# Attention and FFN on one core: another replayed order, and another order of several waits

## The chip, the core and the metric

The kernel runs on one core of one Trainium2 chip. A core has five engines with instruction queues of their own: TensorE (PE in the profile; its weight loads are PEld), VectorE (DVE), ScalarE (ACT), GpSimd (POOL) and SyncE (SP), which here only issues transfers. They meet through semaphores alone. Matrix products land in PSUM, which this kernel uses as eight banks of 512 fp32 columns; everything else lies in SBUF. The metric is the device time of one execution in microseconds, median of several; lower is better.

## What is computed

From the reference, for one sequence of S = 2048 positions with D = 640, 32 heads of 20 columns that share one key and one value head, and F = 1728:

```python
xn = _layernorm(x)
q = (xn @ wq).reshape(B, S, 32, 20)          # 32 query heads
k, v = xn @ wk, xn @ wv                      # one head for all
p = _softmax(einsum("bhqd,bkd->bhqk", q, k) * 20 ** -0.5)
a = einsum("bhqk,bkd->bhqd", p, v) ... @ wo
f = silu(xn @ w1) @ w2
return x + a + f
```

## The kernel before

**Tiling.** Queries are cut into 4 chunks of 512 columns, heads into 8 groups of 4, keys into 16 tiles of 128. So there are 32 (chunk, group) pairs with 16 key tiles of 4 heads each: 2048 score tiles of 128 keys x 512 queries. A score tile is one matmul with 32 rows (L1211); four of them, one for each head, run side by side in the four row groups of PE. A PV step multiplies the exponentials of one key tile with v for 4 heads, side by side in four column groups (L1336); it sums into the bank of its group.

**Two ways to an exponential.** The ACT path: one ACTIVATE (L1301, "exp") reads one to three neighbouring banks and writes bf16. The DVE path, for whole key tiles: a conversion on DVE (L1533, "p1") for each of the 4 heads turns scores into integers whose bits are an approximate exponential; two integer shifts of the whole tile (128 x 2048) give two more approximations, each on POOL (L1572) or on DVE (L1577); three PV steps, one for each with its own scaled copy of v, then sum them. So a tile on the DVE path needs 4 conversions, 2 shifts and 3 PV steps, one on the ACT path 4 banks of exp and 1 PV step.

**Jobs.** Between the attention run the other products as jobs, all with matmuls of L536 in four column groups: "q" (queries of a later chunk, 5 pieces a chunk, one DVE copy, then DMAs that spread its rows over heads), "h" (FFN up, 14 pieces a chunk, the last one shared by two chunks; a tanh on ACT at L862 and a product on DVE at L865), "out" (FFN down and attention output, half a token tile, 320 columns, one DVE operation at L992), and for the last chunk "y", "w", "sum", "spread" and "fin".

**Where the order comes from.** `build` does not write instructions. It makes operations (`Op`) with an estimated duration and a list of what they wait for, and a planner commits them one by one to the five engines; `emit` then writes the queues. Until 36 us of planned time, `step_pe` chooses by rules. From there on (`replay["on"]`), `follow` (L2094) reads the string `ORDER` (L116), three letters a step, which fixes what PE does next, and `follow_other` the strings `OTHERS` (L180), which fix the order of the kinds of operations on ACT, DVE and POOL. In `ORDER`, `S`/`s` is a score set for ACT (second letter: number and spacing of banks; third: first bank), `D` to `K` one score tile for DVE (head, bank; the letter also says which shifts go to DVE), `a`/`d` a PV step of ACT's or of DVE's path, `n` the start of a job, `m` its next matmuls. When the string ends, the rules decide the rest.

**Durations in the planner.** `t_act`, `t_dve`, `t_mc` (L250 ff.) and the tables `WAY*`, `*_END`, `SWITCH` estimate how long operations and the ways between engines take. In the replayed part the estimates do not choose what comes next on PE; they decide, in `est` and `commit`, when an operation is thought to start and end, and with it how the queues of SP and the unlisted operations fall in.

**Waits.** `emit` keeps for each engine what it already knows of the others and writes the missing waits ahead of an operation, in a list sorted by the position of the awaited operation in its own engine's queue, last first (L2306). An instruction carries one wait, and further ones become semaphore instructions ahead of it, which the profile shows at L2339.

Of the kernel before, what the change touches and what calls it, by code (L numbers as in the profile page):

```python
# [10 lines left out]
I16 = mybir.dt.int16  # L11
# [9 lines left out]
HG = 4  # L21
# [30 lines left out]
WAY = {("act", "dve"): 32.0, ("dve", "pool"): 84.0, ("pe", "act"): 41.0, ("pe", "dve"): 72.0}  # L52
# [5 lines left out]
ACT_END = 104.0  # L58
DVE_END = 85.0
# [22 lines left out]
SWITCH = {"s": 97.0, "p": 98.0, "f": 98.0}  # L82
SPRIO = 0.5
# [28 lines left out]
def rule(n):  # L112
# [4 lines left out]
    "D32D13S14a97nq6m00m00D25S20m00m00S22D34aa7S20Dd5nh6m00D04D22S13m00m00m00S20S14Dd5G33nh2m00m00m00m00S25D00D31nh4m00m00m00m00ab7S25D20S13nh2m00m00m00m00"  # L117
    "S25Dc1D14nh0m00m00m00m00ac7S21D23s25ad7ae7af7d04d14S31D30d34d24D85D16S17a04d44d64S10S21D33d54a14d94S25E20D97d74dc4S22D01d84df4S25D20D97a24da4nh1m00S22"
    "E30m00D05D26S17m00m00S22E30a34a44db4S25Dc7di4dd4S22D20dl4nh1m00S35de4S10D32Dc3m00m00dg4dj4m00S25E12S17nq0m00m00m00m00dh4S22D35D81a54a64S26D10a74S22D75"
    "nh1m00m00m00m00S25D20S17nh2m00m00dk4m00m00S25D11S13dm4nh7m00m00m00dn4m00S30D85G26nh3m00m00m00m00S24D27s20D12a06a16a26a36d06S24D33Da7d16d36S20D02d26d66"  # L120
    "S23D35a46d46S20E12D87a56d96d56S33D32d86S20D17a66dc6nh2m00S23Dc5D77m00m00m00da6S20E25d76nh3m00m00S24Dc7m00S20D12m00a76nq7m00S24D72m00m00db6m00S20D23a86"
    "S24D82a96df6S20D13E27de6dd6nh2S24D33m00D10E21S17m00m00m00S33S10nh7dh6m00m00m00dg6m00S11S24Db3a02a12d02d32d12S20D13D26d62d22S24D07a22a32S13S20Da6a42d52"
    "nh7m00m00S23D05D16m00m00a52d92d82S20D33De4a62S25d42d72da2S20D33De7dc2S25D04a72nh3m00S20D77m00S24E16m00m00S17D10De1a82db2S24E06a92dd2S20D17de2nh3m00S24"
    "D06m00m00aa2m00S26S10Da1F34nh5m00m00m00m00S22D06a07d07d37S20D34d27d17S22D15a17d67S20Da4D36d57d97S22D05a27d77S20Da4nh6m00m00S22D15m00a37S20D34d87D05E12"
    "S13m00nh4m00m00S20Dd5a47m00m00S22D06d47a57dc7S20D26Dd5da7df7S22E34db7S20D26a67dd7S24D02nh3m00m00S20Dd6m00a77S24E32de7dg7m00S20D26a87nq2m00m00S25D04m00"
    "m00S20D93a97dh7d04S25D32d14S20D23a04d34d24S25D02E37d64S20D93a14nh2m00S25D07m00D23S10D81m00m00a24S35D33nh0m00m00m00m00a34d54S31s25D17d94d74dc4d84d44D20"
    "S21E33a44da4Dc7S25D10a54db4S21D23nh7m00E35Dc0S16m00m00m00S21D13a64df4S25D30dd4nh3m00S21E27m00Dc0S15D26a74m00m00S21D17a84de4S25D30nh7m00S21D83m00m00S25"
    "D20a94dh4S31dg4m00a05d05d35d65D14s16S31nq0m00m00m00m00S26D34a15d25S21D90D23a25d15d45D04S26d55d95S20D92D63a35d75S26D34d85nq2m00S20Dd3m00S26D04m00m00S20"
    "D63a45a55S26E32D04dc5da5db5S20Dd2D63a65df5S26E34nq2m00S20Dd3m00m00S26D04m00a75S20D63a85dd5S26E32de5dg5S20D94a95dh5S22D06E37nq4m00S20D25m00m00S22D06m00"
    "a07d07S20D95d37d67S22D34D06d27S20D25a17a27S32G36d57a37d97S20S25d87dc7a47d17S22Da4F00D11d47d77a57S24Dc6G30S22da7D11S24Dc6a67df7D20s31db7S24D56a77E30s31"  # L130
    "Dc6de7D20S24G36a87S30a97dh7S34dd7dg7nq3m00m00m00m00S20D22a07d07S25D14D83a17d37S20D32d17d47S25D14D83a27d27S20D22d67E34s25D13a37d57S20D22d97a47S23D85G36"
    "S20D22d77da7a57S23D15dc7S20E36d87S22Dc4D15a67df7S20D26db7S22Dc4D55a77S20S16F34a87S22D25de7S20E34F86D15dh7S32a97dd7S20dg7d06d36S32D35G27a06a16S20D95d66"
    "S22D04D37d16no5m00m00m00S20E24m00m00S22D87m00m00m00D14S20m00m00m00d26m00S22S14D87m00m00m00m00m00a26a36S30D33m00a46a56d96d56S24D27d46S20D32Dc3d76da6d86"
    "S24D12E27a66dc6S20D33db6S24D12no7m00m00m00m00S20Dc3m00m00m00m00S24E22a76S20D33m00m00m00m00m00m00S32D25m00m00m00m00a86a96S20E15df6S22Da4D37dd6dg6S20D05"
    "no4m00de6S22Da7m00m00dh6S20D15m00m00m00m00S22D37Da6m00m00m00a05m00S20D07m00a15S22D76d05d15S20D17d35d25S22Da6m00m00a25S20D07m00m00m00m00S22D76a35d65S20"
    "E14D07d55d45S22De6a45a55S20E14D07a65d95S22D36d75d85S20E14Dc7dc5da5S22D26df5db5D14S20D87a75a85a95no2S23E36de5S20D17m00m00m00m00m00S23S26m00m00m00m00m00"
    "m00dh5S20D23D34m00m00m00m00dd5S26D83m00m00m00S20D24dg5a03S26D12a13a23a33S20E34Da5d03d33S26D02a43d13S20D34d63S35E12a53d23nq4m00S20Dc2m00m00m00S25D17d93"
    "d53S20D32d73dc3d43S24D26Dd7a63D00S11S12a73da3d83S24D26a83S20E37Dc2db3nq6m00S24D17m00m00m00S30D87a93aa3S24D26de3no7m00m00m00S30D56m00m00m00m00m00m00m00"
    "S24D36m00m00m00S20D22m00m00dd3S24E36m00m00m00S20D92a03d03d33S24D06d13d23S20D27D92a13a23S34a33d43S20D37D22a43d63d93d53S24D06Dd7a53d73S20E32da3dc3S24D06"
    "a63d83S20D27E32df3no6m00m00m00S24Dc7m00m00S20D22m00m00m00S24D17m00m00m00m00db3S30E37m00m00m00m00m00m00S24D97a73S20D06D32a83dd3no7de3S24E26m00m00S20D82"  # L140
# [12 lines left out]
    "dg0no3m00m00m00S21D87m00m00m00S24D26m00m00S21D57m00m00m00m00dh0S34D37m00m00m00m00m00m00a00S21D27s25E33D84a10a20a30a40S21D13D27d00d30S25E34d10d20S21Dd3"
    "D27d60d40S25D04d90d50S21Dd3a50a60S24E36D07dc0d70d80S21D23a70S34nq7m00m00m00m00S21E33a80db0S24Dc6D17a90D23S11S12da0dd0de0S24D86D57no1m00m00m00m00m00S22"
    "D36m00S24D87m00m00m00m00m00m00S22S16D37m00m00m00m00m00m00aa0S32E25a07a17d07d37S20D16d27d67S22D24E35a27d17S20D86a37d47S22D24D35d57d97S20E16a47d77S22De4"
    "dc7d87S20D06D15a57df7S22D34no6m00db7S20Dc5m00m00m00m00a67S22S24m00m00m00m00m00m00de7S20D22D33m00m00m00m00da7S24E12m00m00m00S20Da3a77a87S24D02D16a97dd7"
    "S20E33dg7no2m00m00S25D84m00m00S20D23m00m00m00dh7m00S34D13m00m00m00S20D37m00m00m00m00m00m00m00S33Da6a07a17a27d07S20D02d37d17S23D35d67d27S20E12D86a37a47"
    "S24D23d97d57d47S20D12Dc6a57d77S24D33d87dc7S20D12Dc6a67da7S24D23df7db7S20D52nq6m00S24E33m00m00m00S20Dc2a77S23D25a87de7dd7S30D56a97E35D24S13dg7no6m00m00"
# [91 lines left out]
def t_act(n):  # L250
    return 64.0 + 0.8333 * n
# [6 lines left out]
def t_mc(n):  # L258
    return n / 2.4 + (9.0 if n >= 512 else 4.0)
# [44 lines left out]
class Sched:  # L304
# [42 lines left out]
    def turn(self, mode):  # L347
        return SWITCH[mode] if mode != self.pe_mode else 0.0

# [2057 lines left out]
```

## Time and profile before

| | us |
|---|---|
| median of 3 runs | 671.09 (670.93 to 672.82) |
| profiled execution, its own time | 671.75 |
| its span, first to last instruction | 669.9 |
| PE busy, 9919 matmuls | 660.0 |
| ACT busy, 750 instructions | 652.7 |
| DVE busy, 1103 instructions | 632.8 |
| POOL busy, 322 instructions | 535.5 |

The profile is of one execution. A busy time is the union of an engine's instructions, which overlap at their ends: neighbours on ACT by some 0.15 us, on DVE by some 0.08. So a busy share near 100% does not tell how much waiting is left; steps from start to start do. "Stretches" are rows of busy time by engine between two times. "The chain" follows the last instruction back to whatever released each step.

### The profile page before, as it was taken

The page shows a single profiled execution, that of the slowest core. Times are in us where ns is not written, and L with a number is a line of the kernel's source. Part 1 is how long each engine was busy: PE and PEld are TensorE (multiplying, and loading weights), DVE is VectorE, ACT ScalarE, POOL GpSimd, SP SyncE. Part 2 cuts the span into 40 slices and gives each one's busy share as a digit, 9 for nine tenths or more (in the row PEclk, how much of TensorE's full clock was granted, in tenths as well). Part 3 has the DMA queues.
Part 4 walks back from the last instruction along what each step waited for, and adds up shares of the span by engine and source line. Part 5 has one row for each costly group of instructions (what it writes and reads, how often), then busy time and mean ns, then how long its engine had stood idle before and what let it go on. Part 6 is the DMA issues. An engine that isn't in the chain of part 4 may idle for free.

```text
span 669.9 us, 22826 instructions
## 1 busy us (share of the span) xinstructions
PE 660.0 (99%) x9919; PEld 240.1 (36%) x9919; DVE 632.8 (94%) x1103; ACT 652.7 (97%) x750; POOL 535.5 (80%) x322
## 2 busy tenths in 40 slices
PE   8999999999999999999999999999999999999997
PEld 5433332332223333333332333333333333344434
DVE  7899999999999999999999999999999999988885
ACT  6999999999999999999999999999999999999995
POOL 6647879888777888977889788878878888778863
PEclk9999999999999999999999999999999999999999
DMA  8652202222131223223222231122422202242021
GB/s 229 169 198 19 30 18 23 23 27 31 26 35 24 34 19 40 30 31 37 63 23 26 26 40 26 24 32 33 77 21 24 21 21 33 22 79 24 9 23 41
DMA packets 34242, 28.99 MB, mean 43 GB/s; under 512 B 15486, under 2 KB 29662, under 8 KB 34142
## 3 DMA queue, kind: packets, MB, share of 16 engines
q1 hardware_dynamic: 33854, 27.20, 26.6%
q8 instruction: 78, 1.28, 0.8%
q10 hardware_dynamic: 288, 0.33, 0.1%
q14 instruction: 22, 0.18, 0.1%
HBM read 11.09 MB, written 2.62 MB: 20 GB/s over the span
## 4 chain that ended last, share of the span: by engine, by line
PE 79%; ACT 10%; DVE 8%; POOL 1%; issue 0%; DMA 0%; DVEq 0%; POOLq 0%; ACTq 0%
PE psall L1336 28%; PE psall L1211 25%; PE psall L536 24%; ACT sbt L1301 9%; DVE sbt L1533 5%; DVE sbt L1577 1%; POOL sbt L1572 1%; PE psall L710 1%; PE psall L684 1%; DVE sbt L782 0%; DVE sbt L1385 0%; DMA sbt<-in_A_x_dram 0%; PE psall L1150 0%; PE psall L1132 0%; DVE sbt L1100 0%
## 5 line engine op out<-in xcount | busy, mean ns | idle before, releaser
L1301 ACT ACTIVATE sbt<-psall 128x1024 bf16<-128x1024 f32 (+2 forms) x677 | 622.7, 1042 | 3.7 <-PE psall L1211 2.7
L1572 POOL TENSOR_SCALAR sbt<-sbt 128x2048 int16<-128x2048 int16 x250 | 474.3, 1897 | 94.3 <-DVE sbt L1577 25.1
L1533 DVE TENSOR_SCALAR sbt<-psall 128x512 int16<-128x512 f32 x720 | 458.1, 681 | 21.0 <-PE psall L1211 16.4
L1336 PE MATMUL psall<-sbt 128*32 128x512 bf16 x3488 | 274.4, 384 | 0.8 <-POOL sbt L1572 0.2
L1211 PE MATMUL psall<-sbt 32*128 32x512 bf16 x2048 | 251.1, 384 | 2.8 <-ACT sbt L1301 1.1
L536 PE MATMUL psall<-sbt 128*32 128x512 bf16 (+4 forms) x3904 | 216.9, 331 | 0.1
L1211 PEld LDWEIGHTS psall<-sbt 32*128 32x128 bf16 x2048 | 69.1, 91 | 222.0 <-ACT sbt L1301 137.3
L536 PEld LDWEIGHTS psall<-sbt 128*32 128x32 bf16 x3904 | 84.5, 95 | 82.6 <-issue 40.2
L1336 PEld LDWEIGHTS psall<-sbt 128*32 128x32 bf16 x3488 | 71.0, 94 | 108.3 <-issue 73.9
L1577 DVE TENSOR_SCALAR sbt<-sbt 128x2048 int16<-128x2048 int16 x110 | 74.6, 710 | 0.2
L949 POOL TENSOR_TENSOR sbt<-sbt 128x512 bf16<-128x512 f32 x30 | 38.3, 1275 | 19.6 <-DVE sbt L1577 17.3
L865 DVE SCALAR_TENSOR_TENSOR sbt<-sbt,psall 128x512 bf16<-128x512 bf16 x52 | 35.2, 677 | 0.2
L862 ACT ACTIVATE sbt<-psall 128x512 bf16<-128x512 f32 x52 | 32.9, 633 | 0.0
L1385 DVE COPY sbt<-psall 128x512 f32<-128x512 f32 x31 | 21.2, 682 | 0.8 <-PE psall L1336 0.6
L782 DVE TENSOR_SCALAR sbt<-psall 128x512 bf16<-128x512 f32 x20 | 13.6, 680 | 0.5 <-PE psall L536 0.3
L661 POOL TENSOR_TENSOR sbt<-sbt 128x2 f32<-128x2 f32 x8 | 5.7, 708 | 8.6 <-DVE sbt L659 8.2
L992 DVE SCALAR_TENSOR_TENSOR sbt<-psall,sbt 128x320 bf16<-128x320 f32 x24 | 11.6, 485 | 0.6 <-PE psall L536 0.6
L674 POOL TENSOR_SCALAR sbt<-sbt 128x640 bf16<-128x640 bf16 x12 | 10.4, 874 | 1.5 <-DVE sbt L666 1.5
L652 DVE BATCH_NORM_STATS2 sbt<-sbt 128x6 f32<-128x320 bf16 x14 | 6.6, 473 | 2.0 <-DMA sbt<-in_A_x_dram 1.9
L684 PE MATMUL psall<-sbt 128*128 128x128 bf16 x80 | 6.9, 220 | 1.1 <-DVE sbt L677 1.1
L1835 PE MATMUL psall<-sbt 128*32 128x256 bf16 x144 | 6.8, 353 | 1.2 <-DVE sbt L576 1.2
L696 DVE COPY sbt<-psall 128x640 bf16<-128x640 bf16 x14 | 6.4, 482 | 1.0 <-PE psall L684 1.0
(59 smaller groups left out, 97.8 us busy)
## 6 DMA issues: line engine op xcount, KB each, us to landing
sbt<-sbt SPq DMA_DIRECT2D x120, 64.0 KB, 3.8
sbt<-in_A_x_dram SPq DMA_DIRECT2D x28, 160.0 KB, 3.9
sbt<-sbt SPq DMA_DIRECT2D x213, 20.0 KB
out_dram<-sbt SPq DMA_DIRECT2D x14, 160.0 KB, 1.9
sbt<-in_B_w_dram SPq DMA_DIRECT2D x1, 2160.0 KB, 12.2
sbt<-in_B_w_dram SPq DMA_DIRECT2D x1, 2080.0 KB, 8.1
sbt<-sbt SPq DMA_DIRECT2D x75, 8.0 KB
sbt<-in_A_wq_dram SPq DMA_DIRECT2D x1, 800.0 KB, 6.3
```

The source lines that it names most:

```text
L536: ins = pe.matmul(ps[j * SLOT:(j + 1) * SLOT, b * BANK + off:b * BANK + off + n], w[:, j * SLOT:(j + 1) * SLOT], x, start=start, stop=stop ...
L782: op = Op("dve", lambda v: v.tensor_scalar_mul(q_st[:, st, :], bk(job.bank), QSCALE), t_dve(512), DVE_END, pre=[job.ready], writes=[res("q ...
L862: t = Op("act", lambda a: a.activation(t_buf[0:rows, ts, :], bk(job.bank, 0, QW, rows=rows), AF.Tanh, scale=0.5), t_act(512), ACT_END, pre ...
L865: u = Op("dve", lambda v: v.scalar_tensor_tensor(out=hT[par][0:rows, fk, :], in0=t_buf[0:rows, ts, :], scalar=1.0, in1=bk(job.bank, 0, QW, ...
L949: nm = pool(lambda e: e.tensor_tensor(oU[:, us, :], U_sb[:, us, :], Rrep, ALU.mult), 1356.0, POOL_END, pre=[uc] + lc + pack_op.get(divmod( ...
L1211: return pe.matmul(bk(b), kT_rep[i * SLOT:(i + 1) * SLOT, kt * P:(kt + 1) * P], qT[i * SLOT:(i + 1) * SLOT, g % NQ, :], start=True, stop=T ...
L1301: return a.activation(Ebuf[:, es * QW:es * QW + w], ps[:, buf[0] * BANK:buf[0] * BANK + w], AF.Exp, scale=ESCALE)
L1336: ins = pe.matmul(ps[i * SLOT:(i + 1) * SLOT, ub * BANK:ub * BANK + QW], lhsT, rhs, start=(first and k < HG), stop=(last and k >= len(lst) ...
L1385: return v.tensor_copy(U_sb[:, us, :], bk(ub))
L1533: p1 = Op("dve", lambda v: v.tensor_scalar(z16[:, i * QW:(i + 1) * QW], bk(job.bank), ZBIAS, 0.0, ALU.add, ALU.max), t_dve(QW) + 2.0, DVE_ ...
L1572: op = pool(lambda v, t=t, j=j, zin=zin: v.tensor_scalar(t.bitcast(I16), zin, float(SHIFT[j]), 1.0, ALU.add, ALU.mult), POOL_SHIFT, POOL_E ...
L1577: op = dve(lambda v, t=t, j=j, zin=zin: v.tensor_scalar_add(t.bitcast(I16), zin, float(SHIFT[j])), t_dve(N, 4), prio=SPRIO - 0.01 * j, **args)
```

## The change

Three things change.

1. **`ORDER` and `OTHERS` are other strings**, 3128 steps instead of 3144. What they hold, counted:

| in the replayed part | before | after |
|---|---|---|
| score sets for ACT of 1 / 2 / 3 banks | 88 / 504 / 62 | 76 / 528 / 54 |
| banks on the ACT path | 1282 | 1294 |
| score tiles on the DVE path | 716 | 704 |
| shifts on DVE / on POOL | 110 / 250 | 105 / 249 |
| PV steps, ACT's / DVE's path | 323 / 540 | 326 / 531 |
| job starts and further job steps | 109 + 802 | 108 + 801 |

One "fin" piece that stood in the string is left to the rules behind its end. `q`, `h` and `out` jobs start at other places.

2. **The planner has a second set of durations** for the replayed part (`HOT`), and a step letter `r` (one row of a job's matmul among score tiles), which the new string does not use.

3. **`emit` sorts the waits that it writes** by the planned end of the awaited operation, latest first. What is known to be waited for is found as before.

```diff
-WAY = {("act", "dve"): 32.0, ("dve", "pool"): 84.0, ("pe", "act"): 41.0, ("pe", "dve"): 72.0}
+WAY = {("act", "dve"): 32.0, ("dve", "pool"): 84.0, ("pe", "act"): 42.0, ("pe", "dve"): 72.0}
+WAY_HOT = dict(WAY)
+WAY_HOT["dve", "pool"] = 130.0
...
+ACT_HOT = 150.0
...
+HOT = {"on": False}
+FIRST = 10.0
...
 ORDER = (
-    "D32D13S14a97nq6m00m00D25S20m00m00S22D34aa7S20Dd5nh6m00D04D22S13m00m00m00S20S14Dd5G33nh2m00m00m00m00S25D00D31nh4m00m00m00m00ab7S25D20S13nh2m00m00m00m00"
...
+    "a97D32s23D16nq5m00m00S20D22m00m00S23Dc6aa7ab7S20D32nh5m00S14D13D36m00m00m00S30D23nh4m00m00m00S13Dc6m00S20D12ac7S25D33ad7nh2m00E24S10Dc1m00m00m00S25S13"
...
 def t_act(n):
-    return 64.0 + 0.8333 * n
+    return (57.0 if HOT["on"] else 64.0) + 0.8333 * n
...
 def t_mc(n):
-    return n / 2.4 + (9.0 if n >= 512 else 4.0)
+    return n / 2.4 + (3.0 if HOT["on"] else 9.0 if n >= 512 else 4.0)
...
     def turn(self, mode):
-        return SWITCH[mode] if mode != self.pe_mode else 0.0
+        return (106.0 if HOT["on"] and mode == "s" else SWITCH[mode]) if mode != self.pe_mode else 0.0
...
         if e == "pe" and not replay["on"] and not replay["at"] and ORDER and sc.t["pe"] >= HAND and cur_job[0] is None and not pro:
+            HOT["on"] = True
             replay["on"] = True
...
                 items = sorted(req.items(), key=lambda kv: -kv[1][1].seq)
+                found = []
                 for k, (v, d) in items:
                     if know.get(k, 0) >= v:
                         continue
                     s = dma_sems[k[1]][0] if k[0] == "d" else esem[k[1]]
-                    prog[e].append(("w", s, v))
+                    found.append((d.fin, s, v))
                     know[k] = v
                     for kk, vv in clock[d].items():
                         if know.get(kk, 0) < vv:
                             know[kk] = vv
+                for _, s, v in sorted(found, key=lambda x: -x[0]):
+                    prog[e].append(("w", s, v))
```

More of the change, by code (lines that the diff above doesn't have):

```diff
@@ new lines @@
+    "D34ae7af7d00d10d30S14D11s25E27d20d60S23D82a00d40S25D21D37d50d90S23E12a10d70dc0S25Da1D37d80df0S23D02a20nh1S25Da7db0m00S22D14a30m00m00m00S24S16D37de0di0"
+    "da0nh3dd0m00S21D14De5m00m00m00S26E04a40a50S21D15dh0dl0S26D03E34dj0S21D95a60nq3m00S26D04m00dk0S21D25m00m00S26E34a70dg0S21D95nh3m00m00S26S14m00S21D25m00"
+    "dn0dm0S26a04a14a24d04D05D30s21d34d14S26D83D15a34d24d64S20D22E33d54S25D87a44nh2m00S20D23d94S25D17m00m00S13D30Dd1m00a54d74S35D00nh3d84m00m00m00m00S20D22"
+    "s25Dc7a64a74dc4db4S20D32D23d44D17S25a84nh2m00S20E33m00m00S25Dc7a94dd4S20D23de4da4S25D17aa4m00S20E33d07d37S25D84a07nq3m00m00S20D22m00m00D14S25a17d67S22"
@@ new lines @@
+    "D30Da1d17d27S24D06a27d97S20D32Da3d57nh6m00S24E12m00S20D33d87m00d47m00a37S24s20De2a47d77dc7D03S24D16a57da7S20D32nh3m00S14D05E16m00m00m00S20S12De5a67df7"
+    "db7S24D06de7a77S20D32De3nh6m00m00S24E12a87S20D33dg7m00m00S24D02E13dh7dd7S20a97d02d32S14S15D86d62a02S20D23D37nh4m00m00S25D13m00S20Da7a12d22d92m00d52S25"
+    "D03s20D37a22d12d42E14S25a32nh3m00S20Da7d82m00S24D06a42dc2S20D37m00da2S24D16a52d72Dc7D10s11m00df2S24S16Dc7nh1m00m00m00a62m00S24D20a72db2S26D53s10S24D31"
+    "de2dg2a82S26D23D90dd2nq1m00S24E33m00S26D20m00m00S23D05a92E30s26S11dh2a05d05d35d65S23D80s26D22a15nh1m00m00m00m00S23D10a25S26E32d15d45d75d25S20D84D13a35"
@@ new lines @@
+    "d95S26D22s14d55S10D81D53a45nh2m00S26D31D24m00m00m00S20Dc3a55d85S26E34dc5db5S20D12Dc3a65df5S26D24nh2m00S20D53m00E34S16D27m00m00S20E33a75dd5de5S26D94a85"
+    "D03S30dh5nh4m00m00S26D23a95da5S20D82dg5m00m00S26D33a02d02a12S20D15d32d22S26D23E34d62nh5m00S20D83a22S26D24d52d92S20D13a32d72m00S26D34d12m00m00S20D83a42"
+    "d42S26D24dc2d82D13S20Dc5a52nh4m00S26E33m00S20D15a62db2S13D27E36m00m00S20Dc5nh7m00m00m00m00S25D13df2dd2de2S20S13Dc4a72S26D25a82S20D54dh2a92da2dg2D33S26"
+    "nq5m00S20D84m00m00m00S22D26a07d07S20D54a17d37S22D36D25d27S14S10D81a27d47d67S25E32D23nh4m00m00S20D12a37S25E33d97d57S20D82a47dc7m00S25D23m00S20D12d77d17"
@@ new lines @@
+        "eeeeeeeeeeeeeeeeeeeeeeeeeeeeeeeeeeeeeeeeeeeeeeeeeeeeeeeeeeeeeeeeeeeeeeeeeeeeeeeeeeeeeeeeeeeeeeeeeeeeeeeeeeeeeeeee"),
+    "dve": (
+        "gggpppqppppphpphppppuhpppppppppppsshpppphppppsppqppsspuhpppppppppppphsphpppppspppuphppqppppppsspphppppppphpppppsphpupppppsshpppppsppppphhphpspppppqppu"
+        "ssppphppppppppphpppppppphppssppuphpppppssppphpppppppphphpssppuppqpppppppppsppphppphpppppsssspuhpppqppppppppphpppppppphpppqpppppsssppouppppppppppppppps"
+        "sspppoppusppppppqpspppspppppoppppppupssppopppppppppppppppqpppsssuppoppppppppppsppqppppppsssopppppupppppopsppppppppppspppppsoppupppshpppppsppphppppppss"
+        "phppuhphpppppppsphpppphppppphpphphpppppqpsshpuhpphpppppqpppppppppppqppppppsssuqppppppppppsopppppppppsspppupoppppppppppppsspqpspppspppoppupqspppppppppp"
+        "ppppppsspppoppppussppppppspppoppppppppsppppuppppoppppppppssspqpssppppuppopqppppppppppspppsppoppppppppupppppppphppphppssphppppphppsshpphpphuphpphsppppp"
+        "ppppppppsshpphpphphuphhpppppppspopppppppppppppppsssopuppppppsppppoppppppppsspppppoppupsspppopppppppppoppppspppsuopppppppoppsppppppyppspuppppppyppppppp"
+        "spypppppppupppppywpwpppwppwppsspupppppypsppppspppsgw"),
@@ L202 @@
+        "ppdddpppppdpppdppdppdppdpppddpppppdppppppppddppppppppppdddppppdpppddppppppddpdpdpppdpppppddpppddppdppppdppppppdddpddpppppppdpdpppppppppddpppddppppdppp"
+        "pddpppppppdpppppdddpppdppppddppppddppppppdpdpppppdppppdppppppdpppppppppppddpppdpdpdp"),
 }
@@ L385, in commit @@
                 start += self.turn(op.mode)
+                if HOT["on"] and op.mode != "s":
+                    op.occ += FIRST
                 self.pe_mode = op.mode
@@ L524, in dve, with act @@
         return sc.add(Op("dve", fn, occ, lat, **kw))
-    def act(fn, occ, lat=ACT_END, **kw):
-        return sc.add(Op("act", fn, occ, lat, **kw))
+    def act(fn, occ, lat=None, **kw):
+        return sc.add(Op("act", fn, occ, (ACT_HOT if HOT["on"] else ACT_END) if lat is None else lat, **kw))
     def pool(fn, occ, lat=10.0, **kw):
@@ L993, in out_job @@
                                                         in1=xres[:, i, e0:e1], op0=ALU.mult, op1=ALU.add),
-                t_dve(HALF) + 40.0, DVE_END, pre=[job.ready, xres_op[(qc, i)]] + [norm_op[n] for n in range(NT)], reads=[res("xres", i)], writes=[res("os", sl) if hf == 0 else res("os2", sl)],
+                t_dve(HALF), DVE_END, pre=[job.ready, xres_op[(qc, i)]] + [norm_op[n] for n in range(NT)], reads=[res("xres", i)], writes=[res("os", sl) if hf == 0 else res("os2", sl)],
                 prio=0.3, job=job, on_commit=com)
@@ L1349, in f @@
             return pv_mms(pe, flags["bank"], lst, flags["first"], flags["last"])
-        op = Op("pe", f, 224.0, pre=[x[1] for x in d.values()] + v_op[kt // 4],
+        op = Op("pe", f, t_mc(QW) if HOT["on"] else 224.0, pre=[x[1] for x in d.values()] + v_op[kt // 4],
                 reads=[res("E", x[0]) for x in d.values()] + [res("vv", kt // 4, 0)],
@@ L1576, in dve_advance @@
             else:
[L1577 removed]
+                op = dve(lambda v, t=t, j=j, zin=zin: v.tensor_scalar_add(t.bitcast(I16), zin, float(SHIFT[j])), t_dve(N, 4) + (10.0 if HOT["on"] else 0.0),
                          prio=SPRIO - 0.01 * j, **args)
@@ L1589, in f @@
                 return pv_mms(pe, flags["bank"], lst, flags["first"], flags["last"])
-            pv = Op("pe", f, 224.0, pre=pre + v_op[kt // 4], reads=rd + [res("vv", kt // 4, j)],
+            pv = Op("pe", f, t_mc(QW) if HOT["on"] else 224.0, pre=pre + v_op[kt // 4], reads=rd + [res("vv", kt // 4, j)],
                     mode="p", prio=1.5, name=f"PVd{g}_{kt}")
@@ L2090, in finished @@
                 and all(not sc.pools[e] for e in sc.ENG))
+    HOT["on"] = False
     replay = {"on": False, "at": 0, "st": None, "act": 0, "dve": 0, "pool": 0, "port": 0}
@@ L2140, in follow @@
             op, what = cur_job[0].mms[0], ("mm", None)
+        elif k == "r":
+            piece = cur_job[0]
+            rest = piece.job.rest
+            full = a != "h"
+            x = next((x for x, v in rest.items() if b in v and (len(x.rows) == HG) == full), None)
+            if x is None:
+                x = next((x for x in piece.mms if (len(x.rows) == HG) == full), None)
+            if x is None or x.cut is None or not all(p.done for p in x.pre):
+                return None
+            row = row_op(piece.job, x, b)
+            op, what = row[0], ("row", row)
         elif k == "n":
```

139 lines of the change are left out of this document (58 added, 81 removed).

## The prediction

> **What bounds the kernel now.** I read the page first (busy shares, chain of waits), then the busy time by stretches, the chain inside the odd stretch, single rows for prices, and last the waits.
>
> ```profile
> span 669.9 us, 22826 instructions
> ...
> PE 660.0 (99%) x9919; PEld 240.1 (36%) x9919; DVE 632.8 (94%) x1103; ACT 652.7 (97%) x750; POOL 535.5 (80%) x322
> ...
> PE 79%; ACT 10%; DVE 8%; POOL 1%; issue 0%; DMA 0%; DVEq 0%; POOLq 0%; ACTq 0%
> ...
> L1533 DVE TENSOR_SCALAR sbt<-psall 128x512 int16<-128x512 f32 x720 | 458.1, 681 | 21.0 <-PE psall L1211 16.4
> ```
>
> Three engines are over 94% busy, so no one of them is "the" bound: PE, ACT and DVE hand banks of PSUM to each other all the time, and whichever has most to do in a stretch sets that stretch. POOL has a fifth of the span free and 1% of the chain, and the chain holds no DMA: they decide little. The replayed part of the order runs from 36.9 us to the last PV matmuls at 661.1 us. Below are its first four stretches, cut after every 40 us of work for PE (by the prices further down), then the whole; the two pairs behind it are the same view of the third and fourth for L1533 alone (the conversions of the DVE path) and for L536 alone (matmuls of the q, h and out jobs).
>
> ```profile
> core 0: us, PE busy (x) PEld busy (x) DVE busy (x) ACT busy (x) POOL busy (x), PEclk, DMA share, GB/s
> 36.90:78.20 41.30, 41.21 (x581) 13.67 (x583) 40.91 (x71) 41.26 (x54) 30.33 (x17) 1.00 0.26 63
> 78.20:119.60 41.40, 41.31 (x558) 13.13 (x550) 40.98 (x70) 41.30 (x52) 34.86 (x20) 1.00 0.23 23
> 119.60:161.70 42.10, 42.08 (x563) 12.86 (x559) 41.73 (x71) 42.10 (x51) 36.05 (x20) 1.00 0.20 24
> 161.70:207.40 45.70, 44.18 (x510) 13.08 (x506) 45.50 (x78) 45.70 (x49) 36.70 (x20) 1.00 0.31 36
> 36.90:661.30 624.40, 621.39 (x9308) 217.63 (x9310) 599.07 (x1000) 622.08 (x710) 512.53 (x280) 1.00 0.25 33
> ```
>
> ```profile
> 119.60:161.70 42.10, 30.91 (x50) 1.00 0.20 24
> 161.70:207.40 45.70, 35.73 (x59) 1.00 0.31 36
> ```
>
> ```profile
> 119.60:161.70 42.10, 14.52 (x196) 4.13 (x196) 1.00 0.20 24
> 161.70:207.40 45.70, 5.15 (x72) 1.34 (x68) 1.00 0.31 36
> ```
>
> One stretch stands out: the fourth took 45.7 us for the same 40 us of PE work. It holds 72 job matmuls where the third has 196, and 59 conversions where that has 50: jobs ran out, attention filled PE, and attention is what loads ACT and DVE. The chain there lies on DVE and POOL:
>
> ```profile
> 174.17 3.59 DVE sbt L1533 x6
> 177.75 1.20 DVE sbt L1577 x2
> ...
> 179.82 1.90 POOL sbt L1572
> ```
>
> The granted clock is 1.00 in every row, so it enters no term.
>
> **The change part by part.** Prices first: two rows of PE in the chain near the end, two of ACT's timeline without idle time between them, and two groups.
>
> ```profile
> 642.58 0.98 PE psall L1336 x16
> 643.56 0.33 PE psall L1211 x4
> ```
>
> ```profile
> 354.75 5.62 ACT L1301 ACTIVATE sbt<-psall 128x1024 bf16<-128x1024 f32 x6
> ```
>
> ```profile
> 360.22 1.98 ACT L1301 ACTIVATE sbt<-psall 128x1024 bf16<-128x1024 f32 x2
> ```
>
> ```profile
> L862 ACT ACTIVATE sbt<-psall 128x512 bf16<-128x512 f32 x52 | 32.9, 633 | 0.0
> ...
> L992 DVE SCALAR_TENSOR_TENSOR sbt<-psall,sbt 128x320 bf16<-128x320 f32 x24 | 11.6, 485 | 0.6 <-PE psall L536 0.6
> ```
>
> PE: four sets of four matmuls, one turn among them, take 0.98, a lone score set with its turn 0.33; three more sets are 0.65, so one takes some 0.215, and each turn between score sets and the others 0.11. ACT: from 354.75 to 360.22 six exps of two banks began, 5.47 / 6 / 2 = 0.456 us a bank. (An exp lasts longer than that, because neighbours overlap: the 5.62 are five steps of 0.91 and a last one of 1.06.) A tanh costs its 0.633 less the same overlap of 0.15, say 0.49. DVE: 3.59 / 6 and 1.20 / 2, so 0.60 for a conversion and for a shift, likewise for its other 512-wide work; for L992 0.485 less the 0.08 that separates 0.68 from 0.60, so 0.40. A 320-wide set of PE is put at 320/512 of 0.215.
>
> Counted over both order strings, the work that one engine gets: exps 655 to 659 with 1282 to 1294 banks, so ACT +12 x 0.456 = **+5.5 us**. Conversions 716 to 704 and DVE shifts 110 to 105: DVE -12 x 0.60 - 5 x 0.60 = **-10.2 us**. POOL's shifts 250 to 249. PE: PV sets 863 to 857 (-1.3 us), score sets 605 to 606 (+0.2), stretches of score sets 572 to 575 with two turns each (+0.7), one job piece put behind the order (-0.4): **-0.8 us**. So nobody's load falls where all three are short: DVE's load moves to ACT.
>
> Where it lies counts for more. I cut both orders after every 40 us of PE work, gave each piece these prices, and took the longest of the three engines in each (PE / ACT / DVE us):
>
> | piece | before | measured | after |
> |---|---|---|---|
> | 1 | 40.2 / 40.0 / 40.9 | 41.3 | 40.2 / 41.3 / 41.7 |
> | 2 | 39.9 / 40.9 / 40.0 | 41.4 | 40.0 / 42.6 / 40.6 |
> | 3 | 40.3 / 41.3 / 40.6 | 42.1 | 40.0 / 43.6 / 43.0 |
> | 4 | 39.8 / 46.1 / 46.3 | 45.7 | 39.9 / 43.0 / 41.2 |
> | 5 to 13 | 359.9 / 365.6 / 349.9 | 371.4 | 360.0 / 367.0 / 342.0 |
> | rest | 81.0 / 77.0 / 60.2 | 82.5 | 80.1 / 78.9 / 59.1 |
>
> The peak of piece 4 goes (46.3 to 43.0), pieces 1 to 3 take it back (+0.8, +1.7, +2.3), as their jobs move to piece 4 and attention fills their place. The answer hangs on the cut, that is, on how far engines can run ahead of each other. Sums of the longest, averaged over shifted cuts: 80 us pieces 616.2 to 618.4 (+2.2), 40 us 618.4 to 619.7 (+1.3), 20 us 624.4 to 623.6 (-0.8), 10 us 640.1 to 638.4 (-1.7). The 20 us cut gives the measured 624.4, so I take **-0.8**, with +2.2 and -1.7 as its ends.
>
> The jobs that move take their DMAs along: each q job issues pieces of 20 KB on SP's queue, behind the la/lb/lc and pack transfers of the norm steps.
>
> ```profile
> sbt<-sbt SPq DMA_DIRECT2D x120, 64.0 KB, 3.8
> ...
> sbt<-sbt SPq DMA_DIRECT2D x213, 20.0 KB
> ```
>
> ```profile
> 660.65 0.61 PE L536 MATMUL psall<-sbt 96*32 96x512 bf16 x8
> ...
> 661.53 0.66 ACT L1434 ACTIVATE sbt<-psall 128x256 f32<-128x256 f32 x2 [0.50 <-PE psall L1336]
> ```
>
> Their number stays, a landing takes some 4 us against queries needed pieces later, and the chain has 0% DMA: nothing, hidden behind attention already queued; without that cover one 3.8 us landing. The job piece put behind the order (L536 at 660.65, two sets, 0.43 us) then falls where PE waits for the copy on ACT at 661.53: between 0 and +0.43, I take +0.2, since other pieces stand there already. The new durations in the planner emit no instruction; they act through the order alone.
>
> **The wait order.** An instruction carries one wait; each further one is a semaphore instruction ahead of it (L2339):
>
> ```profile
> L2339 PEldq EVENT_SEMAPHORE  x104: 51/51/51, 9.2 to 660.0; - x104
> ```
>
> ```profile
> 253.56 0.40 PE L1336 MATMUL psall<-sbt 128*32 128x512 bf16 x4
> ...
> 253.98 0.13 PEld L1211 LDWEIGHTS psall<-sbt 32*128 32x128 bf16 x4 [0.32 <-DVE sbt L1533]
> 254.01 0.40 PE L1211 MATMUL psall<-sbt 32*128 32x512 bf16 x4
> ```
>
> In the program's list the first wait is the one that the instruction carries. On PE the semaphore instruction mostly waits for ACT and the load carries the wait for DVE. Where ACT is last, as at 253.98, the set begins 0.45 after the PV set at 253.56 instead of the 0.33 of the rows above. Counting the records, 21 of the 91 such cases after 36 us start their load at once when the semaphore instruction is through; the others wait for PE itself. Putting the late wait on the load saves between the 51 ns of that instruction and 0.12 us: 1.1 to 2.5 us on PE, zero if ACT's next work is late for another reason. I take **-0.8**. Behind a waiting load stand all of PE's later sets, so this is on the path; on DVE and POOL the same saves little, as their waits end behind idle time or queued work.
>
> The Trainium skill (Perfetto Trace Analysis, Sequencer Loop) has engine instructions wait in a queue while the sequencer reads on, and control instructions execute in the sequencer itself. By it every one of the 104 would hold up what follows, a case taken up below; the trace agrees for 21 of 91.
>
> The sum: -0.8 + 0.2 - 0.8 = -1.4 us. The profiled execution took 671.75 (span 669.9 and 1.85 around it) and would take 670.35; it lies 0.66 above the median 671.09, so the forecast is **669.7 us**, with 667.0 to 673.7 as its own range (from -1.7 + 0 - 2.5 to +2.2 + 0.4 - 0).
>
> **The rivals.** *Shorter waits inside the pieces.* The 80 us cut says 616.2 of work on the longest engine against 624.4 measured: 8.2 us are lost to fine hand-offs. A search with better durations could win two thirds, 5.5: **665.6 us**. For it: a new search can place each score set anew. Against it: the new order leaves ACT less room, 624.4 less its 616.5 us of work is 7.9, where it had 624.4 - 611.1 = 13.3.
>
> *Every semaphore instruction counts.* If all 104 on PE cost their 51 ns, the sort gains 5.3 instead of 0.8: 671.09 - 0.8 + 0.2 - 5.3 = **665.2 us**. Against it stand the 70 of 91 loads that start later for another reason.
>
> *ACT sets the pace.* ACT is the longest engine in pieces 2, 3 and 4 of the new order and over the nine pieces after them (367.0). If its 13.3 us without new work stay (hand-offs it does not control), its 5.4 more come on top: +5.4 + 0.2 - 0.8 = +4.8, **675.9 us**. It decides as soon as ACT's waits shrink by less than those 5.4. For it: ACT waits for PE's next score set in saturated stretches too; against it: 4 us of the waits lie where PE alone is long (the rest: 81.0 against 77.0), and there the new order gives ACT more to do.
>
> *Nothing happens*: same order in effect, late waits already in front: **671.1 us**.
>
> **How the numbers follow.** A measurement of this kernel tells a change from none at about 0.3%, 2.0 us: faster is below 669.1, slower above 673.1. Forecast 0.37 (0.11 of it below 669.1, 0.03 above 673.1), shorter waits 0.24 (0.23 faster, 0.01 same), every semaphore instruction 0.05 (faster), ACT's pace 0.27 (0.26 slower, 0.01 same), nothing 0.07 (same). Faster 0.39, same 0.32, slower 0.29. The range goes to the fast rivals and to ACT's pace: 664.0 to 676.0.
>
> **What would show it.** Stretch 161 to 207 level with its neighbours, with more job matmuls there and fewer before: right on the peak. L1301 at 681 and L1533 at 708 instructions: the counts. Pieces 1 to 4 at some 42 to 43 us each: ACT and DVE took the peak back; at 41: the first rival. PE's L1211 steps of 0.45 behind semaphore instructions on ACT gone: the sort. A total under 667.0 or above 673.7 makes the forecast wrong; ACT's steps between exps tell which way.

## The result, and the profile after

The changed kernel takes **672.44 us** (median of 22 runs, 672.26 to 673.32), the kernel before beside it 671.23 (22 runs): ratio 1.0016 [1.001, 1.0022]. That is 1.2 us slower, a sixth of a per cent, inside the 0.3% that the prediction called no change, though these many runs tell it apart. The forecast of 669.7 had the wrong sign. Of the executions whose granted clock is on record, 35 of 145 with the old strings ran at 0.996 or 0.997 and took 1.1 to 1.7 us longer, none of 83 with the new strings did, and "at equal clock" below means medians without them: 671.08 for the kernel before and 672.44 for the changed one, 1.4 apart.

The page of the kernel after (its lines stand 7 further down: L1301 is L1308, L1533 is L1540, L1211 is L1218, L1336 is L1343, L536 is L543):

```profile
span 670.5 us, 22744 instructions
...
PE 661.5 (99%) x9892; PEld 239.4 (36%) x9895; DVE 625.7 (93%) x1086; ACT 654.4 (98%) x754; POOL 533.6 (80%) x321
...
PE 60%; ACT 36%; DVE 3%; DMA 0%; issue 0%; POOL 0%
...
L1308 ACT ACTIVATE sbt<-psall 128x1024 bf16<-128x1024 f32 (+2 forms) x681 | 628.3, 1101 | 2.4 <-PE psall L1218 2.0
...
L1540 DVE TENSOR_SCALAR sbt<-psall 128x512 int16<-128x512 f32 x708 | 454.5, 685 | 28.9 <-PE psall L1218 23.0
```

The counts are those forecast (681 and 708). DVE is 7 us less busy; its part of the chain goes from 8% to 3%, ACT's from 10% to 36%. The busy time by stretches of the kernel after, its first four pieces of 40 us of PE work and the whole replayed part:

```profile
core 0: us, PE busy (x) PEld busy (x) DVE busy (x) ACT busy (x) POOL busy (x), PEclk, DMA share, GB/s
36.90:79.20 42.30, 42.22 (x553) 13.14 (x548) 41.43 (x72) 42.30 (x53) 33.52 (x18) 1.00 0.27 61
79.20:121.90 42.70, 42.48 (x540) 12.99 (x540) 41.85 (x71) 42.70 (x55) 35.15 (x20) 1.00 0.27 27
121.90:165.70 43.80, 43.43 (x540) 13.69 (x532) 43.40 (x74) 43.80 (x55) 36.35 (x20) 1.00 0.21 22
165.70:208.40 42.70, 42.40 (x533) 12.76 (x533) 41.59 (x71) 42.70 (x53) 36.73 (x21) 1.00 0.23 26
36.90:661.60 624.70, 622.99 (x9279) 216.91 (x9278) 591.20 (x983) 623.77 (x714) 510.64 (x279) 1.00 0.25 32
```

The peak of piece 4 is gone: 45.7 us before, 42.7 now. Pieces 1 to 3 took it back: 41.3, 41.4 and 42.1 became 42.3, 42.7 and 43.8. ACT is busy for the whole of each of the four, but so it nearly was before (41.26 of 41.30 us in the first), so this column does not tell the two apart. L1540 and then L543 alone, third and fourth piece, show how level the mix has become (conversions were 50 and 59, job matmuls 196 and 72):

```profile
121.90:165.70 43.80, 33.09 (x52) 1.00 0.21 22
165.70:208.40 42.70, 32.44 (x52) 1.00 0.23 26
```

```profile
121.90:165.70 43.80, 11.87 (x160) 3.49 (x160) 1.00 0.21 22
165.70:208.40 42.70, 12.27 (x160) 3.14 (x160) 1.00 0.23 26
```

The two chains side by side. In the chain of before, the 195 longest links hold two stretches of ACT's exps behind 30 us:

```profile
30.98 1.93 ACT sbt L1301 x2
...
352.51 57.36 ACT sbt L1301 x60
```

In the chain of after ACT stands at nearly every place up to 180 us, and again from 351 us on; four of its links:

```profile
48.10 9.23 ACT sbt L1308 x11
...
122.13 10.23 ACT sbt L1308 x12
...
163.84 14.30 ACT sbt L1308 x17
...
351.74 72.36 ACT sbt L1308 x78
```

These shares are a hint and no more: with the old strings ACT's share of the chain was 10% in this execution, but 25% in that of `sort_only`, 22% in that of `old_order_hot` and 31% in that of `before_dve10` (all below), in which neither ACT nor PE has less to do.

**The profiled execution of before holds a hiccup.** It lay 0.66 us above its median. A timeline of it around 287 us shows where that came from: a product on POOL (L949, which scales a group's sums by their reciprocals after DMAs have spread these) waits 1.07 us, by the trace for a DMA, and PE's score set at 290.77 has idled 0.92:

```profile
286.49 1.27 POOL L949 TENSOR_TENSOR sbt<-sbt 128x512 bf16<-128x512 f32 x1 [1.07 <-DMA sbt<-sbt]
...
290.77 0.10 PEld L1211 LDWEIGHTS psall<-sbt 32*128 32x128 bf16 x3 [0.92 <-DVE sbt L1533]
```

With the same order in another execution (the first experiment below) there is no such wait, and the same set has idled 0.34:

```profile
285.32 1.27 POOL L949 TENSOR_TENSOR sbt<-sbt 128x512 bf16<-128x512 f32 x1
...
289.82 0.10 PEld L1211 LDWEIGHTS psall<-sbt 32*128 32x128 bf16 x3 [0.34 <-DVE sbt L1533]
```

In all five other profiled executions with the old strings, the exps behind this place start 0.7 to 0.8 us earlier against this execution than the exps ahead of it do. So the replayed part of before takes some 623.7 us where nothing is late (624.4 less 0.7), against 624.7 after: 1.0 us. Another 0.3 lies behind the last PV step: 669.9 - 661.3 = 8.6 us before, 670.5 - 661.6 = 8.9 after; but in `sort_only` and `old_order_hot` this end is 0.1 to 0.2 longer than in before too, so it is some 0.1 to 0.3. Pieces 1 to 4 together went from 170.5 to 171.5 us, but where a piece ends rests on the prediction's prices, and a small error in them moves the ends by as much; so the levelling of the four is safe to read, and where in the order the 1.0 us was lost is not.

### The profile page after: what moved, and what is told of

The parts are those of the page before. It is cut to its first block, busy times and chain, and to the rows that moved or that the text cites. A ratio compares the mean times of both kernels' runs of the same rounds, so it can differ in the third digit from the quotient of the medians.

```text
span 670.5 us, 22744 instructions
## 1 busy us (share of the span) xinstructions
PE 661.5 (99%) x9892; PEld 239.4 (36%) x9895; DVE 625.7 (93%) x1086; ACT 654.4 (98%) x754; POOL 533.6 (80%) x321
## 4 chain that ended last, share of the span: by engine, by line
PE 60%; ACT 36%; DVE 3%; DMA 0%; issue 0%; POOL 0%
ACT sbt L1308 33%; PE psall L1343 21%; PE psall L1218 19%; PE psall L543 18%; ACT sbt L869 2%; DVE sbt L659 1%; DVE sbt L661 1%; DVE sbt L703 0%; DMA sbt<-in_A_x_dram 0%; PE psall L1139 0%; PE psall L1157 0%; DVE sbt L1107 0%; DVE sbt L663 0%; ACT sbt L648 0%; DVE sbt L666 0%
## 5 line engine op out<-in xcount | busy, mean ns | idle before, releaser
L1308 ACT ACTIVATE sbt<-psall 128x1024 bf16<-128x1024 f32 (+2 forms) x681 | 628.3, 1101 | 2.4 <-PE psall L1218 2.0
L1540 DVE TENSOR_SCALAR sbt<-psall 128x512 int16<-128x512 f32 x708 | 454.5, 685 | 28.9 <-PE psall L1218 23.0
L1343 PE MATMUL psall<-sbt 128*32 128x512 bf16 x3464 | 273.1, 384 | 0.1
L1218 PE MATMUL psall<-sbt 32*128 32x512 bf16 x2048 | 253.1, 384 | 2.8 <-ACT sbt L1308 1.3
L543 PE MATMUL psall<-sbt 128*32 128x320 bf16 (+5 forms) x3904 | 220.4, 331 | 0.0
L1218 PEld LDWEIGHTS psall<-sbt 32*128 32x128 bf16 x2048 | 70.2, 91 | 227.4 <-ACT sbt L1308 165.2
L543 PEld LDWEIGHTS psall<-sbt 128*32 128x32 bf16 (+1 forms) x3904 | 84.3, 95 | 79.0 <-issue 38.7
L1343 PEld LDWEIGHTS psall<-sbt 128*32 128x32 bf16 x3464 | 69.9, 94 | 107.6 <-issue 77.8
L1584 DVE TENSOR_SCALAR sbt<-sbt 128x2048 int16<-128x2048 int16 x105 | 70.6, 702 | 0.8 <-PE psall L1343 0.2
L869 ACT ACTIVATE sbt<-psall 128x512 bf16<-128x512 f32 x52 | 35.8, 688 | 0.0
L681 POOL TENSOR_SCALAR sbt<-sbt 128x640 bf16<-128x640 bf16 x12 | 10.4, 874 | 1.5 <-DVE sbt L673 1.5
L947 DVE RECIPROCAL sbt<-sbt 128x16 f32<-128x16 f32 x30 | 7.3, 244 | 0.0
```

Source lines behind the costliest of these rows:

```text
L543: ins = pe.matmul(ps[j * SLOT:(j + 1) * SLOT, b * BANK + off:b * BANK + off + n], w[:, j * SLOT:(j + 1) * SLOT], x, start=start, stop=stop ...
L869: t = Op("act", lambda a: a.activation(t_buf[0:rows, ts, :], bk(job.bank, 0, QW, rows=rows), AF.Tanh, scale=0.5), t_act(512), ACT_END, pre ...
L1218: return pe.matmul(bk(b), kT_rep[i * SLOT:(i + 1) * SLOT, kt * P:(kt + 1) * P], qT[i * SLOT:(i + 1) * SLOT, g % NQ, :], start=True, stop=T ...
L1308: return a.activation(Ebuf[:, es * QW:es * QW + w], ps[:, buf[0] * BANK:buf[0] * BANK + w], AF.Exp, scale=ESCALE)
L1343: ins = pe.matmul(ps[i * SLOT:(i + 1) * SLOT, ub * BANK:ub * BANK + QW], lhsT, rhs, start=(first and k < HG), stop=(last and k >= len(lst) ...
L1540: p1 = Op("dve", lambda v: v.tensor_scalar(z16[:, i * QW:(i + 1) * QW], bk(job.bank), ZBIAS, 0.0, ALU.add, ALU.max), t_dve(QW) + 2.0, DVE_ ...
```

## The experiments

The kernel before is timed beside each (its median there was 671.11 to 671.61, and 671.03 to 671.09 at equal clock).

**Which part of the change does it?** The change was taken apart. `sort_only` is the kernel before with the new order of waits:

```diff
+                found = []
...
-                    prog[e].append(("w", s, v))
+                    found.append((d.fin, s, v))
...
+                for _, s, v in sorted(found, key=lambda x: -x[0]):
+                    prog[e].append(("w", s, v))
```

> The order of before with the new sort of the waits alone. Theory A (ACT's added banks set the pace, the sort helps a little): 0.3 to 1.5 us faster than before. Theory B (the sort harms: the semaphore instruction that now waits for DVE holds PE's sequencer): 0.5 to 2 us slower. The forecast had -0.8.

Measured: 670.86 us, ratio 0.9987 [0.9977, 0.9997]: 0.4 us less by medians (671.24 before), 0.2 at equal clock (670.82 against 671.03), where the two sets of times overlap. That is not theory B, and at the lower end of theory A or below it.

`order_only` is the changed kernel with these lines taken out again (the old order of waits, the new strings and durations):

```diff
-                found = []
...
-                    found.append((d.fin, s, v))
+                    prog[e].append(("w", s, v))
...
-                for _, s, v in sorted(found, key=lambda x: -x[0]):
-                    prog[e].append(("w", s, v))
```

> The new strings and durations with the waits in the old sort. Theory A: slower than before by 1.5 to 2.7 us, as the whole change (+1.2) lacks the sort's gain. Theory B: 0.8 us faster than before, as the order was forecast, and the sort is what costs.

Measured: 672.69 us, ratio 1.0016 [1.0007, 1.0025]: 1.45 us more by medians (671.24 before), 1.7 at equal clock (671.03 before). This is theory A.

`old_order_hot` is the changed kernel with the old strings:

```diff
 ORDER = (
-    "a97D32s23D16nq5m00m00S20D22m00m00S23Dc6aa7ab7S20D32nh5m00S14D13D36m00m00m00S30D23nh4m00m00m00S13Dc6m00S20D12ac7S25D33ad7nh2m00E24S10Dc1m00m00m00S25S13"
+    "D32D13S14a97nq6m00m00D25S20m00m00S22D34aa7S20Dd5nh6m00D04D22S13m00m00m00S20S14Dd5G33nh2m00m00m00m00S25D00D31nh4m00m00m00m00ab7S25D20S13nh2m00m00m00m00"
...
 OTHERS = {
...
```

> The strings of before in the new planner (its second set of durations and the sort stay). Both theories: within 0.3 us of the run with the sort alone, since durations emit no instruction in the replayed part; if it differs by more, the durations act through the sort or through what the strings leave open.

Measured: 671.18 us, ratio 0.9993 [0.9984, 1.0003]; at equal clock 670.99, against 671.03 before and 670.82 for `sort_only`, within the 0.3 that was expected.

What follows: the new strings cost 1.7 us, and the sort of the waits gives back a quarter of a microsecond (672.69 to 672.44 in the new order; the 0.2 in the old one may be nothing). The new durations alone show nothing that can be told from none.

How the sort works is seen at the set of the prediction's rows (253.56 to 253.98 before). In the timeline of `sort_only`:

```profile
253.41 0.40 PE L1336 MATMUL psall<-sbt 128*32 128x512 bf16 x4
253.77 0.10 PEld L1211 LDWEIGHTS psall<-sbt 32*128 32x128 bf16 x4 [0.26 <-ACT sbt L1301]
253.78 0.39 PE L1211 MATMUL psall<-sbt 32*128 32x512 bf16 x4
```

The set begins 0.37 after the PV set, where it was 0.45, and the load now carries the wait for ACT. But it is in part an exchange. Of the 91 semaphore instructions on PE behind 36 us, 83 waited for ACT before; now 29 do, and 54 wait for DVE. Those whose load starts within 80 ns of them, and which may therefore have held it up, went from 35 to 14 for ACT and from 0 to 16 for DVE. That the planned ends name the wrong one of two waits in such cases is likely, but not shown.

**Is ACT the one that the new strings overload?** In both kernels every exp from number 40 on leaves out its last 10 columns (`n` is the number of the exp):

```diff
-                    return a.activation(Ebuf[:, es * QW:es * QW + w], ps[:, buf[0] * BANK:buf[0] * BANK + w], AF.Exp, scale=ESCALE)
+                    m = w - 10 if 40 <= n < 1000000 else w
+                    return a.activation(Ebuf[:, es * QW:es * QW + m], ps[:, buf[0] * BANK:buf[0] * BANK + m], AF.Exp, scale=ESCALE)
```

In the traces, exps of two banks that follow each other without a wait begin 903 ns apart, and 895 with the cut; with 20 columns less it is 886. So 10 columns are some 8.3 ns, and the cut takes 637 x 8.3 ns = 5.3 us of ACT's work off the kernel before and as much off the changed one (641 exps), while PE and DVE keep theirs. By such steps (476, 903 and 1330 ns for one, two and three banks) the new strings' exps, 12 fewer of one bank, 24 more of two and 8 fewer of three, cost 5.3 us more than the old ones': the cut takes off what the change put on.

> Before, each exp from the 41st on leaves out the last 10 of its columns (8.3 ns each, 637 exps, 5.3 us of ACT work, about what the change added). Theory A (the longest engine of each stretch sets the time; ACT is it more often after the change): 1.5 to 3 us faster. Theory C (hand-offs set the time, not any engine's amount of work): under 1 us.

> After the change, the same 10 columns left out of each exp. Theory A: 3 to 4.5 us faster than the changed kernel, clearly more than the same cut gives before. Theory C: under 1 us, and no more than before.

Measured: before 669.81 us, 0.9977 [0.9968, 0.9986], so 1.35 us for 5.3 of work (671.16 before), between the two theories; after 668.57 us, 0.996 [0.9946, 0.9974], so 3.87 us less than 672.44, as theory A had it. The same cut is worth some three times as much in the new order (5 runs, the longest 669.89), and with it the new order beats the old one by 1.24 us. That each exp ends 8 ns earlier, and its bank comes free earlier, is the same in both orders and can't alone make the difference.

**Does the next cut give as much?** `after_act20` leaves out 20 columns.

> The changed kernel, in which every exponential from number 40 on leaves out its last 20 columns instead of 10: another 5.5 us of ACT's work gone. The first 10 columns gave 3.9 us (672.44 to 668.57). If the price of ACT's work falls as ACT stops being the longest engine, the next 10 give what 10 gave in the kernel before, 1.3 us: about 667.2. If ACT's work is always on the path in the new order, they give 3.9 again: about 664.7. If nothing is left to gain: 668.5.

Measured: 667.98 us, 0.9947 [0.9932, 0.9962]: another 0.6 us only, from 5 runs each that spread over more than that, but far from 3.9. The price of ACT's work falls steeply within 1% of its load, towards what it is in the kernel before or below.

**Where does ACT bind?** The cut was put into the exps 40 to 205 alone (32 columns each, up to the end of piece 4) and into those from 206 on (11 columns each), in the changed kernel, in place of the line of the even cut:

```diff
-                    m = w - 10 if 40 <= n < 1000000 else w
+                    m = w - 32 if 40 <= n < 206 else w
```

```diff
-                    m = w - 10 if 40 <= n < 1000000 else w
+                    m = w - 11 if 206 <= n < 1000000 else w
```

> The changed kernel, in which the exponentials 40 to 205 on ACT (up to about 208 us of the span, pieces 1 to 4) leave out their last 32 columns: 5312 columns less, some 4.4 us of ACT's work, all of it early. If ACT sets the pace over all pieces, the 3.9 us that 6410 columns gave when spread over the whole give here 3.2: about 669.2 us. If ACT sets it in pieces 1 to 4 alone, more than that, up to 4: about 668.5. If it sets it only behind them, under 1 us: about 671.7.

> The changed kernel, in which the exponentials from number 206 on (behind piece 4) leave out their last 11 columns: 5225 columns less, some 4.4 us of ACT's work, all of it late. If ACT sets the pace over all pieces: 3.2 us less, about 669.2. If it sets it in pieces 1 to 4 alone: under 1 us less, about 671.7. If only behind them: up to 4 less, about 668.5.

Measured: early 670.55 us, 0.9988 [0.9978, 0.9998], 1.9 us less than 672.44; late 670.11 us, 0.9978 [0.9968, 0.9987], 2.3 less. Both give something, and neither the 3.2 that proportion asked for: a deep cut in one place runs out of use, as the 20 columns do. The busy time of pieces 1 to 4, first with the early cut, then with the late one (171.5 in the kernel after):

```profile
36.90:206.50 169.60, 168.46 (x2153) 52.00 (x2150) 167.65 (x284) 168.88 (x212) 141.39 (x78) 1.00 0.24 33
```

```profile
37.00:208.50 171.50, 170.53 (x2158) 52.60 (x2153) 168.21 (x284) 171.50 (x212) 141.76 (x78) 1.00 0.24 32
```

The early cut gains its 1.9 inside these pieces and nothing behind them, the late one nothing inside them. So ACT's work is on the path in both parts.

**Are PE and DVE on the path?** DVE: the conversions into the first three z buffers leave out 10 columns after the first 16 tiles (388 and 392 of them; where they follow each other they begin 598 ns apart in full and 587 to 588 with the cut, so some 10.4 ns each and 4.0 us in all).

```diff
-        p1 = Op("dve", lambda v: v.tensor_scalar(z16[:, i * QW:(i + 1) * QW], bk(job.bank), ZBIAS, 0.0, ALU.add, ALU.max),
+        m = QW - 10 if zi < NZ and len(closed) > 16 else QW
+        p1 = Op("dve", lambda v: v.tensor_scalar(z16[:, i * QW:i * QW + m], bk(job.bank, 0, m), ZBIAS, 0.0, ALU.add, ALU.max),
```

> Before, each conversion into the first three buffers (after the first 16 tiles) leaves out the last 10 columns (10.4 ns each, some 4 to 6 us of DVE work). Theory A: 0.7 to 2 us faster, won in the stretch from 162 to 207 us. Theory C: under 0.5 us.

> After the change, the same 10 columns left out of each such conversion. Theory A: under 0.7 us, less than before, since DVE is nowhere the longest engine but in the first and third stretch. Theory C: under 0.5 us in both.

Measured: before 670.85 us, 0.999 [0.9981, 0.9999], 0.3 less (671.16 before), where theory A asked for at least 0.7; after 672.28 us, 1.0012 [1.0003, 1.0022], 0.16 less than without, not to be told from nothing.

PE: the PV matmuls of all groups but the first and the last two leave out 16 columns.

```diff
-            ins = pe.matmul(ps[i * SLOT:(i + 1) * SLOT, ub * BANK:ub * BANK + QW], lhsT, rhs,
+            ins = pe.matmul(ps[i * SLOT:(i + 1) * SLOT, ub * BANK:ub * BANK + QW - cut], lhsT, rhs[:, 0:QW - cut],
```

> The kernel before, in which the PV matmuls leave out their last 16 columns (all groups but the first one and the last two): some 810 sets by 6.7 ns, 5.4 us less work for TensorE, ACT's and DVE's work unchanged. If TensorE is what mostly sets the pace before (79% of the chain): 3 to 4.5 us less, about 667.5. If the three engines set it in turn: 1.5 to 2.5 less.

> The changed kernel with the same cut in the PV matmuls, 5.4 us less work for TensorE. If the pace went from TensorE to ACT with the new order, the gain is smaller than in the kernel before, by 1 us or more: 1 to 2 us less, about 671. If both kernels hang on TensorE alike, the gain is the same as there, 3 to 4.5.

Measured: before 670.3 us, 0.9984 [0.9974, 0.9994], 0.8 less; after 672.08 us, 1.0008 [0.9998, 1.0017], 0.36 less than without, which may be nothing. From the page of the kernel before with this cut:

```profile
PE 60%; ACT 34%; DVE 4%; POOL 1%; issue 0%; DMA 0%; DVEq 0%; ACTq 0%
```

From the page of the changed kernel with it:

```profile
ACT 71%; PE 25%; DVE 3%; DMA 0%; issue 0%; POOL 0%
```

Both gains are below the least that was expected (1.5 and 1). The chain of before had 79% on PE, and 5.4 us off PE bring 0.8 there. That the chain of before with this cut has 34% on ACT says little, since the old strings gave 10 to 31% without it. The prices of a microsecond of work, then:

| us of time for each us of work taken off | before | after |
|---|---|---|
| ACT, first 5.3 us | 1.35 / 5.3 = 0.25 | 3.87 / 5.3 = 0.73 |
| ACT, next 5.3 us | not tried | 0.59 / 5.3 = 0.11 |
| PE | 0.81 / 5.4 = 0.15 | 0.36 / 5.4 = 0.07 |
| DVE | 0.31 / 4.0 = 0.08 | 0.16 / 4.1 = 0.04 |

The intervals of the ratios are some 0.1%, 0.7 us, to either side, so in the changed kernel PE's and DVE's prices may be nothing, while ACT's 0.73 stands well clear.

## Why the prediction was wrong

The measured time lies inside the stated 667.0 to 673.7, but that range holds both signs; the forecast itself was for less time, and it was more.

**The counts, the peak and the take-back** held. Pieces 1 to 3 were to grow by 0.8, 1.7 and 2.3 and piece 4 to shrink by 3.3; they grew by 1.0, 1.3 and 1.7 and it shrank by 3.0. All four are at 42.3 to 43.8 us, as the text said for the case that ACT and DVE take the peak back.

**The sort** was put at -0.8 and gave -0.25 in the new order (672.69 to 672.44) and -0.2 at equal clock in the old one, so it was put three times too large. Its mechanism was seen; that other waits, on DVE, would take the place of some was not. ACT's added work, put at 5.5, is 5.3.

**The fin piece** was put at +0.2, within 0 to 0.43. The time behind the last PV step grew by some 0.1 to 0.3. No run tried it alone.

**The step that failed is the choice of the cut**: "The 20 us cut gives the measured 624.4, so I take **-0.8**". The strings and durations cost +1.7 at equal clock (+1.45 by medians), of which some 0.1 to 0.3 lies behind the last PV step. That leaves +1.4 to +1.6 where -0.8 was forecast: near the 40 us cut's +1.3, and inside the ends given. With the end and the sort's -0.25 it makes the 1.4 by which the changed kernel is slower. That a cut's sum equals the measured time is no evidence for it. The 40 us pieces sum to 618.4 where 623.7 were needed before, and to 619.7 where 624.7 were needed after: 5.3 and 5.0 us in which no engine's work sets the time. The 20 us cut met their size by luck; why it gets the sign wrong, perhaps by counting peaks that the buffers even out, no run shows. What should have been compared is the difference of two orders under each cut, and there the two longer cuts, the only ones below the measured time, both said slower.

**ACT sets the pace** was the right rival in its mechanism, wrong in its size. It said that ACT's 13.3 us without new work stay, so that 5.4 more of it cost 5.4. ACT's room went from 623.7 - 611.1 = 12.6 us (without the late DMA) to 624.7 - 616.5 = 8.2: it shrank by 4.4 of the 5.4, so ACT got most of its new work in where it had waited before. "It decides as soon as ACT's waits shrink by less than those 5.4": so it did, by 1.0 us. That much is arithmetic and would hold whatever the cause; the evidence is in the cuts. With 5.3 us taken off ACT, which then has the work that it had before, the new order runs at 668.57, some 2.3 us below `sort_only` (670.86), the old order with the same sort. So what else the strings change (jobs spread, a lighter DVE, other places of everything) is worth some 2.3 us, and ACT's 12 more banks take more than that back, at a price that is 0.25 for a microsecond in the old order and 0.73 in the new. That the even cut stands for these banks is an assumption; strings with 12 banks fewer at the same places were not made.

**Shorter waits inside the pieces** (665.6) and **every semaphore instruction counts** (665.2) fall with the order's and the sort's own measurements. **Nothing happens** (671.1) lies nearer to the result than the forecast, but the order did act, by more than the noise and the other way.

## What to carry to other kernels

Where three engines are busy for 93% of the time and more, neither the shares of the chain nor the busy shares price their work: the engine with 79% of the chain returned 0.15 us for a microsecond, and the share of another went from 10 to 31% between executions of one order. Cut 1% of the work of one engine at a time, in both versions, and read the prices; a change that moves load from an engine at 0.08 to one at 0.25 needs a gain elsewhere that pays for it, and the price of the one that it loads rises as it goes. A model that is fitted to the total should be asked for differences under several settings, and the one nearest to the total has no special claim.

## What the runs showed of the hardware

**A longer exp without a lower rate.** An exp's duration grows while ACT never waits, without any loss of rate. The instructions of L1308 in the kernel after (duration min/median/max in ns, first and last start), in a window from 351 us and in one from 415 us, both inside the long link of ACT in its chain:

```profile
L1308 ACT ACTIVATE sbt<-psall x8: 1018/1065/1112, 351.6 to 358.0; 128x1024 bf16<-128x1024 f32 x8
```

```profile
L1308 ACT ACTIVATE sbt<-psall x10: 1129/1159/1211, 415.6 to 423.8; 128x1024 bf16<-128x1024 f32 x10
```

The steps from start to start are (358.0 - 351.6) / 7 = 0.91 us and (423.8 - 415.6) / 9 = 0.91 us, while the median went from 1065 to 1159 ns. So the mean of a group is no price there: the page's 1042 ns before and 1101 after do not say that an exp became dearer (two banks take 903 ns from start to start in both kernels); they fit with ACT having less room.

**A short fall of TensorE's clock.** The profiled execution of `old_order_hot` took 672.3 us at a mean granted clock of 0.997. Three rows of its busy time, with the granted clock in the third column from the right:

```profile
186.00:188.00 2.00, 1.68 (x19) 0.55 (x19) 2.00 (x4) 2.00 (x3) 1.53 (x1) 0.99 0.86 70
188.00:190.00 2.00, 2.00 (x19) 0.43 (x20) 1.49 (x3) 2.00 (x3) 0.00 (x0) 0.50 0.68 64
190.00:192.00 2.00, 2.00 (x31) 0.59 (x19) 1.29 (x2) 1.13 (x1) 1.15 (x1) 0.65 0.17 42
```

The exps behind it start some 1.4 us later against the kernel before than those ahead of it. It lies in the old order's piece 4, just behind a stretch in which PE was busy for 1.68 of 2 us; the kernel before has the same stretch (1.59 of 2) and stays at 1.00. So the level order may also spare the kernel this loss, which medians hide, but what sets it off no run here shows.
